# The key sum z of a linear attention: a DMA transpose through DRAM and a VectorE sum in place of two matmuls with ones

## The chip, the cores and the metric

The kernel runs on one core of one Trainium2 chip. The metric is the device time of one execution in microseconds (us), the median of several runs. The core has five engines that run their own instruction streams: TensorE (PE) for matmuls, VectorE (DVE), ScalarE (ACT), GpSimd (POOL) and SyncE (SP), which here only issues transfers (DMAs). PE writes its results to PSUM, which has eight banks of 128 x 512 fp32. "PEld" in the profile is PE's loading of weights, which runs beside its matmuls.

## The reference

An input `x` of 2048 rows (tokens) by 512 goes through two branches, which a gate mixes:

```
qkv = x @ wqkv                       # 32 heads of 16
phi(t) = where(t > 0, t + 1, exp(t)) + 1e-6
kv  = sum over s of phi(k)^T v       # per head, 16 x 16
z   = sum over s of phi(k)           # per head, 16; 512 numbers in all
a   = (phi(q) @ kv) / (phi(q) . z + 1e-6) @ wo
b   = (gelu(layernorm(x)^T-mixed by w1, b1) by w2, b2), transposed back
g   = sigmoid(sum(x * gate_w))
out = g * a + (1 - g) * b
```

The change is about `z`, the sum over all 2048 tokens of phi(k): one row of 512 numbers, which every token's denominator needs.

## The kernel before

Tokens are handled in 16 tiles of 128. All engines' instructions are pinned in program order, so the order in the file is the order on each engine and on each queue. SP issues all but three of the transfers. The transfers take eight completion counters in turn, so that each waits for the eighth transfer before it.

The stages, in the order of PE's work:

- Layer norm of the 16 tiles, and the first half of the token mixing (`accA`, seven banks, `w1A`). SP loads `x`, the weights, and `xT` (x transposed by DMA).
- `kacc`: the keys of each tile, `phi` on ACT (exponential) and DVE. Per tile DVE adds `pk` into `zacc` (L309), which so holds 128 partial sums of z, one for each partition. PE collects `Gps` = x^T phi(k). At the end ACT and DVE evict `G_sb`, and DVE splits `zacc` into two bf16 parts, `z_hi` (L333) and `z_lo` (L334).
- The block loop (from L442, `b` = 0 to 6): seven blocks `accB` of the second half of the token mixing. Between them, in `b` = 0, `kv_blocks` (32 small matmuls, 16 small DVE products with `mask`) and `z_row`; in `b` = 1 `w2_blocks`; in `b` = 0 to 3 the 16 query tiles (`q_tile`, 3, 4, 4 and 5 of them), each four matmuls, an exponential on ACT (L282) and two DVE instructions (L284, L289). Gates follow in `b` = 1 and 2, `gate_odds` in `b` = 2. From `b` = 3 on ACT runs the gelus.
- `z_row` is two matmuls: the 128 x 128 matrix `ones` by `z_hi`, then by `z_lo` into the same bank. That sums over the partitions and leaves the row z on every partition. ACT copies it to `zb` (L354).
- `normalise(t)`, four DVE instructions for each tile (L366, L371, L373, L375), the first of which reads `zb`. Each then stores its tile of `pq` to `q_dram` on SP. After every fourth tile `turn(c)` reads four transposed blocks back into `pqT`. Twelve tiles are normalised ahead of the output loop, four in it. Between them SP also loads the second half of `w2`, in two parts: `load_w2(1, 0)` after tile 2 and `load_w2(1, 7)` after tile 7 (behind `turn(1)`). The first needs the place of `w1B`, which PE gives back with the last `accB`.
- The output loop: groups of 8, 4, 3 and 1 tiles. `y_mm` (14 matmuls for each tile with `w2h`), `a_mm` (4 with `pqT`), `finish` (ACT scales into one of seven `ot` buffers, SP stores it).

All 8 PSUM banks come from one pool and are given out in the order in which they came back.

Of the kernel before, what the change touches and what calls it, by code (L numbers as in the profile page):

```python
# [9 lines left out]
ALU = mybir.AluOpType  # L10
AX = mybir.AxisListType
BF16 = mybir.dt.bfloat16
FP32 = mybir.dt.float32
# [3 lines left out]
def kernel(  # L17
# [13 lines left out]
    nc = tc.nc  # L31
    P = nc.NUM_PARTITIONS
# [7 lines left out]
    S, D = X.shape  # L40
    F = B_w1.shape[1]
    NT = S // P
    ND = D // P
# [19 lines left out]
    work = ctx.enter_context(tc.tile_pool(name="work", bufs=3))  # L63
    dpool = ctx.enter_context(tc.tile_pool(name="dpool", bufs=1, space=bass.MemoryType.DRAM))
    psum = ctx.enter_context(tc.tile_pool(name="psum", bufs=8, space=bass.MemoryType.PSUM))

    def ptile(shape, dt, name):
        return persist.tile(shape, dt, name=name, tag=name)

    def bank(name):  # L70
        return psum.tile([P, SC], FP32, name=name, tag="bank")

    def mm(o, lhsT, rhs, start, stop, **kw):
        tc.keep_in_program_order(
            nc.tensor.matmul(o, lhsT=lhsT, rhs=rhs, start=start, stop=stop, **kw)  # L75
        )
# [13 lines left out]
    zb = ptile([P, D], FP32, "zb")  # L90
# [14 lines left out]
    odds = ptile([P, NT], FP32, "odds")  # L105
    c1 = ptile([P, NT], FP32, "c1")
    c2 = ptile([P, NT], FP32, "c2")
    ones = ptile([P, P], BF16, "ones")
    zacc = ptile([P, D], FP32, "zacc")
    z_hi = ptile([P, D], BF16, "z_hi")  # L110
    z_lo = ptile([P, D], BF16, "z_lo")
    eps_t = ptile([P, 1], FP32, "eps_t")

    nc.vector.memset(eps_t[:], EPS)
# [5 lines left out]
    pin = tc.keep_in_program_order  # L120

    def load(o, i, eng=None, **kw):
        pin((eng or nc.sync).dma_start(out=o, in_=i, **kw))
# [23 lines left out]
    for c in range(NSC):  # L147
        for j in range(ND):
# [3 lines left out]
                transpose=True,  # L152
# [6 lines left out]
    for j in range(ND):  # L159
# [10 lines left out]
        out=mask[:], in_=mask[:], compare_op=ALU.is_gt, fill=1.0,  # L170
# [3 lines left out]
        out=mask[:], in_=mask[:], compare_op=ALU.is_ge, fill=0.0,  # L174
        base=0, pattern=[[-HEAD, 8], [0, HEAD]], channel_multiplier=1,
    )
    nc.gpsimd.memset(ones[:], 1.0)
    nc.gpsimd.memset(prod[:, :, HEAD : HEAD + 1], DEN_EPS)


# [57 lines left out]
    def gate(t):  # L238
        junk = work.tile([P, D], BF16, name="junk", tag="junk", bufs=1)
        tc.keep_in_program_order(  # L240
            nc.vector.tensor_tensor_reduce(  # L241
                out=junk[:], in0=xr[:, t, :], in1=gw_b[:], scale=1.0, scalar=0.0,
                op0=ALU.mult, op1=ALU.add, accum_out=gpre[:, t : t + 1],
            )
        )


    def gate_odds(t0, t1):
        pin(nc.vector.tensor_scalar_min(out=gpre[:, t0:t1], in0=gpre[:, t0:t1], scalar1=60.0))
        pin(nc.scalar.activation(out=odds[:, t0:t1], in_=gpre[:, t0:t1], func=ACT.Exp))  # L250
# [6 lines left out]
    def gelu(acc, j):  # L257
        pin(
            nc.scalar.activation(
                out=uT[:, j, :], in_=acc[:], func=ACT.Gelu_apprx_tanh,  # L260
                bias=b1_sb[:, j : j + 1], scale=1.0,
            )
        )
# [61 lines left out]
    def evict(o, acc, i):  # L325
        if i % 2 == 0:
            pin(nc.scalar.copy(out=o, in_=acc))
        else:
            pin(nc.vector.tensor_copy(out=o, in_=acc))

    for i in range(ND):
        evict(G_sb[:, i, :], Gps[i][:], i)
    pin(nc.vector.tensor_copy(out=z_hi[:], in_=zacc[:]))  # L333
    pin(nc.vector.tensor_tensor(out=z_lo[:], in0=zacc[:], in1=z_hi[:], op=ALU.subtract))  # L334


    def mlp1_block(j):
        acc = bank("accB")
        for t in range(NT):
            mlp1(acc, w1B, (j - NFA) * P, t, t == NT - 1)  # L340
        return acc

    def q_tile(t):
        qacc = bank("qacc")
        for k in range(ND):
            mm(qacc[:], xT[:, k, t * P : (t + 1) * P], wq_sb[:, k, :], k == 0, k == ND - 1)
        phi(pq[:, t, :], qacc)


    def z_row():  # L350
        zps = bank("zps")
        mm(zps[:], ones[:], z_hi[:], True, False)
        mm(zps[:], ones[:], z_lo[:], False, True)
        pin(nc.scalar.copy(out=zb[:], in_=zps[:]))  # L354

# [33 lines left out]
    def kv_blocks():  # L391
        kvps = bank("kvps")
        for j in range(ND):
            for k in range(ND):
                for p in range(0, P, 64):
                    c = j * P + p
                    mm(kvps[p : p + 64, j * 64 : j * 64 + 64], wv_sb[:, k, c : c + 64],
                       G_sb[:, k, c : c + 64], k == 0, k == ND - 1, tile_position=(0, p))

        for j in range(ND):  # L400
            for p in range(0, P, 32):
                r = (p + 32 * j) % P
                pin(
                    nc.vector.tensor_tensor(
                        out=kvbdT[r : r + 32, j, p : p + 32],
                        in0=kvps[p : p + 32, j * 64 + p % 64 : j * 64 + p % 64 + 32],
                        in1=mask[p : p + 32, p : p + 32], op=ALU.mult,
                    )
                )

    def w2_blocks():
        w2ps = [bank("w2ps") for _ in range(ND)]
        for j in range(ND):
            for p in range(0, P, 32):
                r = (p + 32 * j) % P
                mm(w2ps[j][p : p + 32, :], kvbdT[r : r + 32, j, p : p + 32],
                   wo_sb[r : r + 32, j, :], True, True, tile_position=(r, p))
        for j in range(ND):
            evict(W2sb[:, j, :], w2ps[j][:], j)
# [4 lines left out]
    def load_w2(h, f0):  # L424
        if f0 == 0:
            w2s.append(wpool.tile([P, NF, S // 2], BF16, name="w2h", tag="w"))
        load(
            w2s[h][:, f0 : f0 + 7, :],
            w2_view[:, f0 : f0 + 7, h * (S // 2) : (h + 1) * (S // 2)],
        )  # L430

    load_w2(0, 0)
    load_w2(0, 7)

    QB = 4
# [4 lines left out]
    for b in range(NFA):  # L442
        acc = mlp1_block(NFA + b)
        waiting.append((acc, NFA + b))
        if b == 0:
            kv_blocks()
            z_row()
        if b == 1:
            w2_blocks()
        if b < QB:  # L450
            for _ in range(n_q[b]):
                q_tile(qi)
                qi += 1
            for t in gates[b]:
                gate(t)
            if b == 2:
                gate_odds(0, NT)
        if b >= QB - 1:
            for a, j in waiting:
                gelu(a, j)  # L460
            waiting = []
# [27 lines left out]
            mm(yps[:, d0:d1], pqT[:, j, t * P : (t + 1) * P], W2sb[:, j, d0:d1], False, j == ND - 1)  # L489

    def finish(t, yps, d0, d1):
        ot = work.tile([P, D], BF16, name="ot", tag="ot", bufs=7)
        if t < NT - 1:
            pin(
                nc.scalar.activation(  # L495
                    out=ot[:, d0:d1], in_=yps[:, d0:d1], func=ACT.Identity,
                    scale=c1[:, t : t + 1], bias=c2[:, t : t + 1],
                )
            )
        else:  # L500
            pin(
                nc.vector.tensor_scalar(  # L502
                    out=ot[:, d0:d1], in0=yps[:, d0:d1], scalar1=c1[:, t : t + 1],
                    scalar2=c2[:, t : t + 1], op0=ALU.mult, op1=ALU.add,
                )
            )
        load(o_view[:, t, d0:d1], ot[:, d0:d1])
# [3 lines left out]
    for t0, t1 in ((0, 8), (8, 12), (12, NT - 1)):  # L511
        for t in range(t0, t1):
            held[t] = bank("yps")
            y_mm(held[t], t, 0, D)
        for t in range(t0, t1):
            a_mm(held[t], t, 0, D)
            finish(t, held[t], 0, D)
            if late and t % 2 == 1:
                normalise(late.pop(0))
                if not late:  # L520
                    turn(NSC - 1)
    t = NT - 1
    for d0, d1 in ((0, 3 * P), (3 * P, D)):
        yps = bank("yps")
        y_mm(yps, t, d0, d1)
        a_mm(yps, t, d0, d1)
        finish(t, yps, d0, d1)
# [30 lines left out]
```

## Time and profile before

| what | us |
|---|---|
| median of three runs | 163.66 (163.52 to 164.1) |
| the profiled execution | 163.69 |
| its span in the trace | 162.0 |
| PE busy | 158.3 (98%) |
| DVE busy | 116.4 (72%) |
| ACT busy | 52.9 (33%) |
| the two matmuls with ones (`zps`) | start at 61.29 and 61.51 |
| copy of `zps` to `zb` on ACT | 61.93, lasts 0.59 |
| first reader of `zb` on DVE (L366) | 88.97 |

The time of an execution is a little longer than the span, which runs from the first to the last recorded instruction. All times of day below are us from the span's start. The granted TensorE clock is full in all 40 slices of the page. The page's DMA line shows that the transfer engines are idle from about 70 to 90 us, and busy around that.

### The profile page before, as it was taken

Reading aid. Unit: us, or ns where it says so; the run is one execution under the profiler, and the core shown is the slowest. Engines: PE = TensorE matmul, PEld = TensorE weight load, DVE = VectorE, ACT = ScalarE, POOL = GpSimd, SP = SyncE. Lnnn points to the kernel's source line nnn. Section 1 sums busy time; section 2 is a strip of 40 time slices with the busy share of each in tenths; the row PEclk is TensorE's granted clock in tenths of the full one; section 3 lists DMA queues with packets and bytes.
Section 4 is the critical chain, followed back from the end, with each engine's and each line's share of the span. In section 5 each row is a group of like instructions: output and inputs, shape, how many; then the busy total and the mean of one; then the engine's idle time right before and its main releaser. Section 6 shows DMA issues by size and latency. Waiting matters only on the chain.

```text
span 162.0 us, 2203 instructions
## 1 busy us (share of the span) xinstructions
PE 158.3 (98%) x791; PEld 73.2 (45%) x791; DVE 116.4 (72%) x271; ACT 52.9 (33%) x91; POOL 1.7 (1%) x11
## 2 busy tenths in 40 slices
PE   7999999999999999999999999999999999999992
PEld 5344444444444445444444444444444444444452
DVE  2899989999999997895959999999999900000002
ACT  4222258962332125271438521000007501150040
POOL 4000000000000000000000000000000000000000
PEclk9999999999999999999999999999999999999999
DMA  5999997444799679900000107736269646647021
GB/s 142 295 336 341 327 187 162 97 98 103 233 395 375 192 243 385 390 26 0 0 0 0 36 32 233 287 76 183 65 98 318 236 97 206 215 93 146 24 97 32
DMA packets 35094, 27.54 MB, mean 170 GB/s; under 512 B 19084, under 2 KB 31500, under 8 KB 35084
## 3 DMA queue, kind: packets, MB, share of 16 engines
q1 hardware_dynamic: 34880, 27.37, 57.0%
q8 instruction: 6, 0.10, 0.3%
q10 hardware_dynamic: 204, 0.04, 0.1%
q14 instruction: 4, 0.03, 0.1%
HBM read 19.01 MB, written 4.19 MB: 143 GB/s over the span
## 4 chain that ended last, share of the span: by engine, by line
PE 98%; DVE 0%; issue 0%; DVEq 0%
PE yps L75 38%; PE accA L75 15%; PE accB L75 15%; PE qacc L75 9%; PE Gps L75 9%; PE kacc L75 9%; PE warm_ps L75 2%; PE kvps L75 0%; PE zps L75 0%; DVE ot L502 0%; PE w2ps L75 0%; PE vps L75 0%; DVEq L502 0%
## 5 line engine op out<-in xcount | busy, mean ns | idle before, releaser
L75 PE MATMUL yps<-uT,w2h 128*128 128x512 bf16 (+2 forms) x238 | 49.2, 366 | 0.0
L75 PEld LDWEIGHTS <-w2h 128*128 128x128 bf16 x238 | 22.8, 98 | 25.9
L495 ACT ACTIVATE ot<-yps,c,c 128x512 bf16<-128x512 f32 x15 | 11.7, 778 | 46.7 <-PE yps L75 37.7
L75 PE MATMUL accB<-xh,w1B 128*128 128x512 bf16 x112 | 25.0, 379 | 0.0
L75 PE MATMUL accA<-xh,w1A 128*128 128x512 bf16 x112 | 24.7, 382 | 0.0
L502 DVE TENSOR_SCALAR ot<-yps,c,c 128x384 bf16<-128x384 f32 (+1 forms) x2 | 1.1, 543 | 28.9 <-PE yps L75 28.9
L75 PEld LDWEIGHTS <-xT 128*128 128x128 bf16 x128 | 12.4, 98 | 15.1 <-issue 0.2
L75 PEld LDWEIGHTS <-w1A 128*128 128x128 bf16 x112 | 10.9, 98 | 13.4 <-issue 0.5
L75 PEld LDWEIGHTS <-w1B 128*128 128x128 bf16 x112 | 10.9, 98 | 13.2
L75 PE MATMUL kacc<-wk_sb,xT 128*128 128x512 bf16 x64 | 15.8, 379 | 0.0
L75 PE MATMUL Gps<-pk,xr 128*128 128x512 bf16 x64 | 15.8, 379 | 0.0
L75 PE MATMUL yps<-W2sb,pqT 128*128 128x512 bf16 (+2 forms) x68 | 14.6, 366 | 0.0
L75 PE MATMUL qacc<-wq_sb,xT 128*128 128x512 bf16 x64 | 14.5, 379 | 0.0
L282 ACT ACTIVATE e<-kacc 128x512 bf16<-128x512 f32 x16 | 9.2, 598 | 12.7 <-DVE pk L289 6.8
L196 DVE BATCH_NORM_STATS2 stats<-xr 128x6 f32<-128x512 bf16 (+1 forms) x19 | 11.1, 582 | 2.2 <-DMA xr<-in_A_x_dram 2.2
L375 DVE SCALAR_TENSOR_TENSOR pq<-pq,odds,rd 128x512 bf16<-128x512 bf16 x16 | 12.0, 752 | 0.6
L282 ACT ACTIVATE e<-qacc 128x512 bf16<-128x512 f32 x16 | 9.6, 597 | 7.9 <-PE qacc L75 7.3
L284 DVE TENSOR_SCALAR e<-e 128x512 bf16<-128x512 bf16 x32 | 9.2, 287 | 3.9 <-ACT e L282 3.6
L371 DVE TENSOR_REDUCE den<-prod 128x32 f32<-128x544 f32 x16 | 11.5, 720 | 0.6
L289 DVE SCALAR_TENSOR_TENSOR pk<-kacc,e 128x512 bf16<-128x512 f32 x16 | 11.1, 692 | 1.0
L289 DVE SCALAR_TENSOR_TENSOR pq<-qacc,e 128x512 bf16<-128x512 f32 x16 | 11.1, 692 | 0.6
L241 DVE CUSTOM_DVE_ANT_0 junk<-xr,gw_b 128x512 bf16<-128x512 bf16 x16 | 11.0, 690 | 0.5
(57 smaller groups left out, 94.7 us busy)
## 6 DMA issues: line engine op xcount, KB each, us to landing
w2h<-in_B_w_dram SPq DMA_DIRECT2D x4, 1792.0 KB, 8.4
w1B<-in_B_w_dram SPq DMA_DIRECT2D x4, 896.0 KB, 7.1
w1A<-in_B_w_dram SPq DMA_DIRECT2D x15, 224.0 KB, 4.1
xr<-in_A_x_dram SPq DMA_DIRECT2D x16, 128.0 KB, 3.9
q_dram<-pq SPq DMA_DIRECT2D x16, 128.0 KB, 1.8
out_dram<-ot SPq DMA_DIRECT2D x15, 128.0 KB, 1.8
wk_sb<-in_A_wqkv_dram SPq DMA_DIRECT2D x1, 512.0 KB, 7.2
wv_sb<-in_A_wqkv_dram SPq DMA_DIRECT2D x1, 512.0 KB, 13.4
```

The costliest lines, as they stand in the source:

```text
L75: nc.tensor.matmul(o, lhsT=lhsT, rhs=rhs, start=start, stop=stop, **kw)
L196: pin(nc.vector.bn_stats(out=stats[t][:, h, :], in_=xr[:, t, d0:d1]))
L241: nc.vector.tensor_tensor_reduce(out=junk[:], in0=xr[:, t, :], in1=gw_b[:], scale=1.0, scalar=0.0, op0=ALU.mult, op1=ALU.add, accum_out=gp ...
L282: pin(nc.scalar.activation(out=e[:], in_=acc[:], func=ACT.Exp))
L284: nc.vector.tensor_scalar(out=e[:], in0=e[:], scalar1=1.0, scalar2=PHI_EPS, op0=ALU.min, op1=ALU.add)
L289: nc.vector.scalar_tensor_tensor(out=o, in0=acc[:], scalar=0.0, in1=e[:], op0=ALU.max, op1=ALU.add)
L371: pin(nc.vector.tensor_reduce(out=den[:], in_=prod[:], op=ALU.add, axis=AX.X))
L375: nc.vector.scalar_tensor_tensor(out=heads, in0=heads, scalar=odds[:, t : t + 1], in1=rd[:].unsqueeze(2).to_broadcast([P, NH, HEAD]), op0= ...
L495: nc.scalar.activation(out=ot[:, d0:d1], in_=yps[:, d0:d1], func=ACT.Identity, scale=c1[:, t : t + 1], bias=c2[:, t : t + 1],)
L502: nc.vector.tensor_scalar(out=ot[:, d0:d1], in0=yps[:, d0:d1], scalar1=c1[:, t : t + 1], scalar2=c2[:, t : t + 1], op0=ALU.mult, op1=ALU.add,)
```

## The change

`z_hi` and `z_lo` become the two halves of one tile `z_parts`. Right after them (behind `load_w2(0, 7)` on the queues) `z_out` stores this tile to DRAM on ACT's queue, as 256 rows of 512, and SP reads it back in four transposes, so that column d of z lies on one partition with its 256 parts side by side. The two matmuls and ACT's copy are gone. `z_row` now stands at the end of block `b` = 2, after `gate_odds`: DVE sums each group of 256 parts into `z_cols` (128 x 4), SP stores these 512 fp32 numbers to DRAM, where they make a row, and SP loads that row to all 128 partitions of `zb`. The matrix `ones` and its memset on POOL are gone; `ot` has six buffers instead of seven, which makes room for `z_turned`.

```diff
-    ones = ptile([P, P], BF16, "ones")
-    z_hi = ptile([P, D], BF16, "z_hi")
-    z_lo = ptile([P, D], BF16, "z_lo")
+    z_parts = ptile([P, 2, D], BF16, "z_parts")
+    z_turned = ptile([P, ND, 2 * P], BF16, "z_turned")
+    z_cols = ptile([P, ND], FP32, "z_cols")
...
-    nc.gpsimd.memset(ones[:], 1.0)
...
-    pin(nc.vector.tensor_copy(out=z_hi[:], in_=zacc[:]))
-    pin(nc.vector.tensor_tensor(out=z_lo[:], in0=zacc[:], in1=z_hi[:], op=ALU.subtract))
+    pin(nc.vector.tensor_copy(out=z_parts[:, 0, :], in_=zacc[:]))
+    pin(
+        nc.vector.tensor_tensor(
+            out=z_parts[:, 1, :], in0=zacc[:], in1=z_parts[:, 0, :], op=ALU.subtract
+        )
+    )
...
+    zp_dram = dpool.tile([2 * P, D], BF16, name="zp_dram", tag="zp_dram")
+    zr_dram = dpool.tile([1, D], FP32, name="zr_dram", tag="zr_dram")
+
+    def z_out():
+        load(zp_dram[:].rearrange("(h p) d -> p h d", p=P), z_parts[:], nc.scalar)
+        for j in range(ND):
+            load(z_turned[:, j, :], zp_dram[:, j * P : (j + 1) * P], transpose=True)
+
     def z_row():
-        zps = bank("zps")
-        mm(zps[:], ones[:], z_hi[:], True, False)
-        mm(zps[:], ones[:], z_lo[:], False, True)
-        pin(nc.scalar.copy(out=zb[:], in_=zps[:]))
+        pin(nc.vector.tensor_reduce(out=z_cols[:], in_=z_turned[:], op=ALU.add, axis=AX.X))
+        load(zr_dram[:].rearrange("o (j p) -> p (o j)", p=P), z_cols[:])
+        load(zb[:], zr_dram[:].to_broadcast([P, D]))
...
     load_w2(0, 0)
     load_w2(0, 7)
+
+    z_out()
...
         if b == 0:
             kv_blocks()
-            z_row()
...
             if b == 2:
                 gate_odds(0, NT)
+                z_row()
...
-        ot = work.tile([P, D], BF16, name="ot", tag="ot", bufs=7)
+        ot = work.tile([P, D], BF16, name="ot", tag="ot", bufs=6)
```

## The prediction

> **What bounds the kernel now.** I read the page first (shares by engine, and the chain that ended last), then the timeline of PE around the change, then those of DVE and of SP, and last the transfers by window. The chain:
>
> ```profile
> PE 98%; DVE 0%; issue 0%; DVEq 0%
> ```
>
> PE is the bound from end to end: its work follows itself without a hole, so a PE instruction that goes away is worth its own pace, unless a wait that was covered comes into the open. The pace and the place, from PE's timeline:
>
> ```profile
> 60.66 0.69 PE L75 MATMUL kvps<-G_sb,wv_sb 128*64 128x64 bf16 x32
> 61.29 0.39 PE L75 MATMUL zps<-z_hi,ones 128*128 128x512 bf16 x1
> 61.51 0.38 PE L75 MATMUL zps<-z_lo,ones 128*128 128x512 bf16 x1
> 61.73 2.75 PE L75 MATMUL qacc<-wq_sb,xT 128*128 128x512 bf16 x12
> ```
>
> The recorded 0.38 is the length of a pipelined matmul; starts are 0.22 apart. From the first zps to the first qacc is 0.44 us. DVE's timeline, where the sum is put in and where `zb` is first read:
>
> ```profile
> 82.01 0.17 DVE L249 TENSOR_SCALAR gpre<-gpre 128x16 f32<-128x16 f32 x1
> 83.75 0.29 DVE L284 TENSOR_SCALAR e<-e 128x512 bf16<-128x512 bf16 x1 [1.56 <-ACT e L282]
> ...
> 88.97 0.68 DVE L366 TENSOR_TENSOR prod<-pq,zb 128x512 f32<-128x512 bf16 x1
> 89.75 0.72 DVE L371 TENSOR_REDUCE den<-prod 128x32 f32<-128x544 f32 x1
> ```
>
> There is a hole of 1.56 us after gate_odds, in which DVE waits for ACT, and ACT for PE. `zb` is read 6.8 us after that hole opens. SP's timeline:
>
> ```profile
> 56.89 1.04 SPq L123 DMA_DIRECT2D w2h<-in_B_w_dram  x2
> 91.68 5.39 SPq L123 DMA_DIRECT2D q_dram<-pq  x3
> 97.20 0.39 SPq L123 DMA_DIRECT2D w2h<-in_B_w_dram  x1
> 99.27 0.33 SPq L123 DMA_DIRECT2D q_dram<-pq  x1
> 105.17 5.06 SPq L123 DMA_TRANSPOSE pqT<-q_dram  x4
> 110.28 2.03 SPq L123 DMA_DIRECT2D q_dram<-pq  x4
> 113.71 5.03 SPq L123 DMA_TRANSPOSE pqT<-q_dram  x4
> 118.79 1.14 SPq L123 DMA_DIRECT2D w2h<-in_B_w_dram  x1
> 119.98 2.06 SPq L123 DMA_DIRECT2D q_dram<-pq  x4
> 128.89 5.04 SPq L123 DMA_TRANSPOSE pqT<-q_dram  x4
> 133.98 1.05 SPq L123 DMA_DIRECT2D out_dram<-ot  x2
> ```
>
> SP is free from 57.9 to 91.7; from there on it is one chain of stores, transposes and loads, started by `normalise`, and a late start is passed down it whole. What that chain must meet on PE is the price of a late `zb`.
>
> **Part by part.**
>
> *The two matmuls go.* Gain 0.43 us (two at 0.216, the pace of 16 accB in 3.45 us). The chain of waits books them at 0.54, by modelled ends; that is the upper end. The lower end is 0: at 67.86 the first w2ps weight load shows 0.42 us idle, put down to a DVE pq that ended at 67.72, and if PE came there 0.43 earlier and that were a true wait, all would be lost. I don't take it as one: the kvps loads show the same 0.42 before them, under the name of a transfer, so it goes with the change to small tiles. The banks say the same: they are reused in the order given back, and with zps gone w2ps takes two banks of Gps, the one of kvps and the one of the first query tile, whose last DVE read ended at 65.87. Taken: 0.43.
>
> *ACT's copy goes, a store is issued there.* The copy (0.59 at 61.93) sat in idle time. The store waits for z_lo, which ends at 60.48, and takes some 0.4 us of ACT (q_dram issues 0.33 to 0.58). Behind it on ACT is the first query exponential, at 62.79 before, 62.36 then: cover 1.4 us. Cost 0.
>
> *The four transposes on SP* wait for that store, with nothing queued behind them but z_row's own transfers. The store is 256 KB. Alone it would land like a q_dram store, 1.7 us; at worst it lands after the w2h loads, which hold the transfer engines until 69.2, plus 0.7 for its own bytes and 0.4 to land: 70.3. Four transposes at 1.26 of issue each (those of 512 rows; these have 256) put the last issue at 74.1; the pqT rows land 2.5 to 4.5 after issue, so the latest is 78.6. DVE wants them at 81.75: cover 3 us at the worst end, 11 at the best. Cost 0. Without cover DVE would stand ahead of the phis of block 3, and their banks.
>
> *The sum on DVE.* 128 x 1024 elements; the nearest row is the den reduction, 128 x 544 in 0.72, so 1.36 in proportion, 1.2 if some of the 0.72 doesn't grow; a bf16 input could be quicker. With PE 0.43 early, gate_odds ends at 81.75 and the hole closes at 83.32 (ACT shifts too). 81.75 + 1.36 = 83.11: inside. Upper end, twice the row (2.7): phis 1.1 late. The fifth query tile of the block needs the bank of its first: PE took it at 85.68, DVE gave it at 84.77, so 0.9 of cover; the next accB had 0.7 to 0.85. PE would lose 0.2 to 0.4. Taken: 0.
>
> *The row's way to `zb`.* Store and load are in series. The store: 512 elements of 4 bytes. No row has elements so small. From below, the last out_dram store (128 rows of 256 bytes) landed in 1.4. The pqT transposes, 512 packets of 256 bytes, keep the 16 transfer engines busy for about 0.75 us, some 20 ns per packet on an engine; the mean over q1 is 57% of 16 x 162 us by 34880 packets, 42 ns. 32 packets on each engine cost 0.65 to 1.35, and with 0.75 to the first byte and 0.4 from the last (read off a q_dram store) the store takes 1.8 to 2.5. I keep 60 ns for the upper end: 3.1. The load: 256 KB to 128 partitions. The w2h issued at 97.20 moved its first byte 1.15 later and landed 0.6 after its last; with 0.75 for the bytes, 2.5. So `zb` is there at 81.75 + 1.36 + 1.8 to 3.1 + 2.5 + 0.15 for two handovers = 87.6 to 88.9, taken 88.2. DVE is ready for it at 88.97 - 0.43 = 88.54, if the phis are not late. Late by -1 to +0.4: taken 0. What a lateness X would cost: normalise(2)'s store, the w2h load behind it at 97.20, turn(0), turn(1) and the last w2h load at 118.79 all go X later. That last load lands 8.7 after issue, at 127.5; PE wants its first block (f = 7 of tile 8, group from 127.81) at 129.1. So 1.6 us are free, then X counts whole. The other meetings are looser: turn(1)'s last block lands near 120.2 and is wanted at 125; turn(2)'s are wanted at 139.9, the first landed by 131.6; turn(3) starts at 141.36 and is wanted at 152.4.
>
> *The eight counters.* Seven more transfers stand ahead of the q_dram stores. Those that the stores then wait for (w2h of the first half, the z transfers) have landed by 90. Cost 0.
>
> *Six ot buffers.* ACT waited 8.1 us for the eighth `ot` until the first out store landed, at 136.06, since these stores stand behind turn(2). With six the seventh and the eighth wait: 136.06 to 136.84 and on to 137.6. SP takes them up only at some 138.6 and 139.1, and the bank of the eighth is wanted at 155. Cost 0.
>
> *Memset of ones on POOL*: at the start, nobody waits. 0.
>
> Sum, against the profiled execution: 163.69 - 0.43 = 163.26. The median before lies 0.03 lower (163.66), so 163.2.
>
> **A page against this.** The Trainium skill, "DMA: Bandwidth & Descriptors", Specifications, says that below 512 bytes a transfer engine does a read-modify-write. The out_dram rows of 256 bytes, under that limit too, landed in 1.4 us, so the trace shows no price for it; no run here has writes of 4 bytes yet. By the page the store pays for a read as well; if that were once 0.75, the store takes 3.3 and X is some 0.6, still inside the 1.6.
>
> **Rivals.**
>
> 1. *The 4-byte store drags (slower).* Mechanism: the 32 small writes on each engine go one after another, each waiting for its own trip. Price of a trip, from the tail between last byte and landing: 0.4; 32 of them 12.8, `zb` at 99.7, X = 11, loss 9.5: 172.7. Milder, 150 ns each: store 6.0, `zb` at 91.8, X = 3.2, loss 1.6, 164.8. It decides from X = 2.85 (1.6 free, 0.43 gained, 0.82 for 0.5%), which is 8.1 us for both transfers where I have 4.3 to 5.6. For it: nothing in the trace is so small. Against: 256-byte packets run at 20 ns, so they overlap. The page's rule above stands beside this rival: a read-modify-write that does not overlap would be this case.
> 2. *The gain is eaten.* By the w2ps load as above, or by a DVE sum twice as long: 163.4 to 163.7.
> 3. *z_turned late.* Landing after 81.75 holds up DVE ahead of the phis, and from 0.9 us on PE's banks. It needs 3 us more than the worst sum; 2 us beyond that costs some 1.1: 164.3.
> 4. *More is gained than the two matmuls.* Only if the change of tile shape after kvps cost PE something too; the starts, 0.22 apart before and after, show nothing. At 0.54 it is 163.1.
>
> **How the numbers follow.** 0.5% (0.82 us) is about what a measurement of this kernel can tell from no change. The forecast has 0.60, rival 2 0.13, rival 4 at its mild size 0.04, all within 0.5%; beyond 0.5% faster I leave 0.05, for a gain with no row. Rival 1 has 0.14, rival 3 0.04: slower 0.18, and so 0.77 within. The range goes from 162.8 (the upper gain of 0.54, and 0.3 of scatter, as the runs shown spread) to 164.5 (X up to 2.8, the edge of slower); it leaves out the far part of rivals 1 and 3 and the unexplained gain.
>
> **What would show it.** After kvps the next PE group is qacc, 0.22 after the last kvps; every later PE start is 0.43 earlier, with no idle PE. The sum on DVE near 81.8, 1.2 to 1.4 long, no wait on a transfer before it. The first prod at 88.5; if it waits for `zb`, the wait is X, and SP's w2h at 118.79 moves by it. The prediction is wrong if a yps of tile 8 waits for w2h, if DVE waits for z_turned, or if w2ps starts at 67.86 as before.

## The result, and the profile after

The changed kernel takes 170.18 us (median of five runs, 169.94 to 170.41) against 163.54 for the kernel before: 1.0397 times as long, with a 95% interval of 1.0377 to 1.0418. The forecast was 163.2, in a range of 162.8 to 164.5. What happened is of the kind of the first rival: the store of 512 numbers of 4 bytes drags, and `zb` comes too late.

PE is no longer the chain. From the page, section 4 of the changed kernel (shares of the span along the chain that ended last, by engine):

```profile
PE 63%; DVE 17%; DMA 14%; SPq 3%; issue 1%; ACT 0%; DVEq 0%
```

In order of time (start, duration, what), the stretch of that chain where it leaves PE:

```profile
81.61 1.23 DVE z_cols L364
82.84 0.02 issue
82.86 8.39 DMA zr_dram<-z_cols
91.25 0.02 issue
91.27 4.67 DMA zb<-zr_dram
95.94 0.02 issue
95.96 0.70 DVE prod L378
```

The sum takes 1.22 and stands where it was meant to stand. Then 2 KB take 8.39 us to DRAM and the row 4.67 us back. DVE's timeline says what that means for the first normalisation:

```profile
95.96 0.69 DVE L378 TENSOR_TENSOR prod<-pq,zb 128x512 f32<-128x512 bf16 x1 [7.49 <-DMA zb<-zr_dram]
```

DVE had been ready at 88.47; it waits 7.49 us. SP's chain, row by row the one shown of before:

```profile
98.61 5.39 SPq L124 DMA_DIRECT2D q_dram<-pq  x3
104.10 0.39 SPq L124 DMA_DIRECT2D w2h<-in_B_w_dram  x1
106.21 0.34 SPq L124 DMA_DIRECT2D q_dram<-pq  x1
112.16 5.06 SPq L124 DMA_TRANSPOSE pqT<-q_dram  x4
117.27 2.05 SPq L124 DMA_DIRECT2D q_dram<-pq  x4
122.52 5.04 SPq L124 DMA_TRANSPOSE pqT<-q_dram  x4
127.60 0.58 SPq L124 DMA_DIRECT2D w2h<-in_B_w_dram  x1
```

All rows down to the second group of q_dram stores are 6.9 to 7.0 later than before (7.49, less the half microsecond by which PE and DVE came early). The second turn is 8.81 later (122.52 for 113.71), and so is the last w2h load (127.60 for 118.79). PE's timeline shows both arriving too late:

```profile
120.33 3.62 PE L75 MATMUL yps<-W2sb,pqT 128*128 128x512 bf16 x16
125.14 0.39 PE L75 MATMUL yps<-W2sb,pqT 128*128 128x512 bf16 x1 [1.19 <-DMA pqT<-q_dram]
126.45 0.39 PE L75 MATMUL yps<-W2sb,pqT 128*128 128x512 bf16 x1 [0.93 <-DMA pqT<-q_dram]
127.86 0.61 PE L75 MATMUL yps<-W2sb,pqT 128*128 128x512 bf16 x1 [1.01 <-DMA pqT<-q_dram]
129.09 5.19 PE L75 MATMUL yps<-W2sb,pqT 128*128 128x512 bf16 x13 [0.62 <-DMA pqT<-q_dram]
134.12 12.41 PE L75 MATMUL yps<-uT,w2h 128*128 128x512 bf16 x56
```

Tile 4 waits 3.75 us in four pieces for the blocks of turn(1). After that 13 matmuls take 5.19 us, 0.40 each instead of 0.22: the granted clock in the stretch 129 to 134 is 0.54 of full speed. Then the weight loads of tile 8 reach f = 7 and wait for the last w2h load:

```profile
133.90 1.39 PEld L75 LDWEIGHTS <-w2h 128*128 128x128 bf16 x7
135.78 1.19 PEld L75 LDWEIGHTS <-w2h 128*128 128x128 bf16 x7 [0.48 <-DMA w2h<-in_B_w_dram]
```

That load was issued at 127.60, so it landed 8.2 later. (f counts the 14 blocks of `w2h` that each tile needs; blocks 7 to 13 of tiles 8 to 15 come with the last load.) Before, f = 7 of tile 8 started near 129.3 (127.81 and seven times 0.216), with no wait; here it starts near 135.9. The difference is 6.6, and the spans differ by 6.5 (168.5 and 162.0): the last w2h load sets the end.

It does so by a small margin. Without this wait f = 7 would have started near 135.6 (134.12 and seven times 0.216), because the four waits for pqT and the slow clock had already cost PE nearly as much; the page's chain accordingly runs through turn(1) and not through this load. So two late arrivals meet within 0.3 us, and both come from the late start of SP's chain. A quicker PE would only have waited longer at f = 7, and an earlier w2h load alone would have gained 0.3.

### The profile page after: what moved, and what is told of

Same layout as the page of the kernel before. It is cut to its first block, busy times and chain, and to the rows that moved or that the text cites. A ratio compares the mean times of both kernels' runs of the same rounds, so it can differ in the third digit from the quotient of the medians.

```text
span 168.5 us, 2205 instructions
## 1 busy us (share of the span) xinstructions
PE 160.6 (95%) x789; PEld 73.3 (44%) x789; DVE 117.8 (70%) x272; ACT 52.1 (31%) x90; POOL 1.5 (1%) x10
## 4 chain that ended last, share of the span: by engine, by line
PE 63%; DVE 17%; DMA 14%; SPq 3%; issue 1%; ACT 0%; DVEq 0%
PE yps L75 22%; PE accA L75 14%; PE kacc L75 8%; PE Gps L75 8%; PE accB L75 6%; DMA zr_dram<-z_cols 5%; PE qacc L75 4%; DVE pq L387 4%; DVE den L383 4%; DVE prod L378 3%; SPq L124 3%; DMA zb<-zr_dram 3%; DMA w1A<-in_B_w_dram 2%; DMA q_dram<-pq 2%; DVE rd L385 2%; DVE pq L289 2%
## 5 line engine op out<-in xcount | busy, mean ns | idle before, releaser
L75 PE MATMUL yps<-W2sb,pqT 128*128 128x512 bf16 (+2 forms) x68 | 17.8, 409 | 3.8 <-DMA pqT<-q_dram 3.8
L378 DVE TENSOR_TENSOR prod<-pq,zb 128x512 f32<-128x512 bf16 x16 | 11.0, 685 | 7.5 <-DMA zb<-zr_dram 7.5
L75 PEld LDWEIGHTS <-pqT 128*128 128x128 bf16 x68 | 7.0, 106 | 13.8 <-DMA pqT<-q_dram 5.3
## 6 DMA issues: line engine op xcount, KB each, us to landing
xr<-in_A_x_dram SPq DMA_DIRECT2D x16, 128.0 KB, 4.1
q_dram<-pq SPq DMA_DIRECT2D x16, 128.0 KB, 1.9
out_dram<-ot SPq DMA_DIRECT2D x15, 128.0 KB, 1.8
```

Source lines behind the costliest of these rows:

```text
L378: nc.vector.tensor_tensor(out=prod[:, :, 0:HEAD], in0=heads, in1=by_head(zb[:]), op=ALU.mult)
```

## The experiments

Theory 1: the two matmuls were worth what PE's starts say, everything else in the change is hidden, and the loss is the lateness of `zb` passed down SP's chain. Its rivals: the new transfers or the smaller `ot` disturb the rest, or the gain is eaten at w2ps. A second question is why 2 KB take 8.4 us.

### Each part alone

`no_zps`: before, with the matmuls and the copy taken out and nothing put in.

```diff
     def z_row():
-        zps = bank("zps")
-        mm(zps[:], ones[:], z_hi[:], True, False)
-        mm(zps[:], ones[:], z_lo[:], False, True)
-        pin(nc.scalar.copy(out=zb[:], in_=zps[:]))
+        pass
...
+    nc.gpsimd.memset(zb[:], 2048.0)
```

> Before without the two matmuls with ones and ACT's copy: zb is a constant set at the start, so z is left out of the result and nothing is put in its place. This is what the removal alone is worth. Theory 1 (the change's gain is the two matmuls, its loss is the late zb): 0.43 to 0.54 us less than before, 163.0 to 163.2. Rival (the gain is eaten by a wait at w2ps): as before, 163.5 to 163.7.

Measured: 163.51, 0.9982 of before (0.9969 to 0.9995); span 161.4. The gain is there and is small: the median lies above the expected 163.0 to 163.2, and the interval allows a gain of 0.1 to 0.5 us. In the profile kvps starts at 60.47 and the first qacc at 61.09, 0.62 apart where before it was 1.07: 0.45 us. The w2ps group starts at 67.24, so no wait there eats it.

`ot6_alone`: before, with `bufs=6` for `ot`.

> Before with six ot buffers instead of seven, nothing else. Theory 1: the seventh output tile waits like the eighth did, and nobody waits for it: as before, 163.4 to 163.8. Rival (the buffers are part of the loss): 164 or more.

Measured: 163.75, ratio 0.9999 (0.9986 to 1.0012). The buffers cost nothing.

`shadow`: the changed kernel with the whole DMA route kept, but `zb` from the matmuls (`ones` and its memset are back).

```diff
...
-        load(zb[:], zr_dram[:].to_broadcast([P, D]))
+        load(zacc[:], zr_dram[:].to_broadcast([P, D]))
...
+    def z_ones():
+        zps = bank("zps")
+        mm(zps[:], ones[:], z_parts[:, 0, :], True, False)
+        mm(zps[:], ones[:], z_parts[:, 1, :], False, True)
+        pin(nc.scalar.copy(out=zb[:], in_=zps[:]))
...
             kv_blocks()
+            z_ones()
```

> The changed kernel with all its transfers, its sum and its six buffers, but zb again comes from the two matmuls; the row of z that the DMAs bring is loaded to zacc, which nobody reads then. Theory 1: nobody waits for the row, so as before, 163.4 to 163.9. Rival (the new transfers or the sum disturb the other work by themselves): 165 to 170.

Measured: 163.79, ratio 1.0004 (0.9991 to 1.0016). The row of z takes as long as in the changed kernel (store 8.6, load 5.1), and it costs nothing as long as nobody waits for it. SP, which sits behind the store until 91.89, issues the first q_dram store at 92.34 instead of 91.68, and that is hidden too. So the transfers are harmless; the wait is the loss.

### How much for how late

`p1_before_gates2`: in the changed kernel, `z_row` ahead of the two gates of block 2.

```diff
+            if b == 2:
+                z_row()
             for t in gates[b]:
                 gate(t)
             if b == 2:
                 gate_odds(0, NT)
-                z_row()
```

> The changed kernel with z_row ahead of the two gates of block 2 instead of behind gate_odds, so about 1.6 us earlier on DVE. Theory 1: zb is there at 94.4 instead of 95.96, and all of the 1.6 comes back: 168.4 to 168.8. Rival (the loss doesn't hang on when zb comes): 170.2 as the changed kernel.

Measured: 168.96, ratio 1.0318 (1.0299 to 1.0338), span 167.0. `zb` is waited for 5.90 us, 1.59 less; the span is 1.5 less (by the medians 1.2, so that 168.96 lies just above the expected 168.4 to 168.8). Theory 1 holds, nearly one for one. Here too it is w2h that ends the wait: issued at 126.01, and PE stands until 134.30.

```profile
132.04 1.67 PE L75 MATMUL yps<-uT,w2h 128*128 128x512 bf16 x7
134.30 10.75 PE L75 MATMUL yps<-uT,w2h 128*128 128x512 bf16 x48 [0.59 <-DMA w2h<-in_B_w_dram]
```

`p2_after_gates1`: `z_row` a whole block earlier.

```diff
+            if b == 1:
+                z_row()
             if b == 2:
                 gate_odds(0, NT)
-                z_row()
```

> The changed kernel with z_row at the end of block 1 instead of block 2. DVE reaches it at 74.5 and waits for z_turned until about 75.0; 1.2 of sum, 8.4 of store and 4.7 of load bring zb at 89.4, 0.9 after DVE is ready for it. Theory 1: that is within the 1.6 us which SP's chain has to spare, so the gain of the matmuls shows: 163.0 to 163.3, faster than before. If nothing is to spare: 164.0. Rival (not the lateness): 170.

Measured: 163.45, ratio 0.9984 (0.9972 to 0.9995), span 161.6. DVE still waits 0.93 us for `zb`, and PE for nothing; the gain of the matmuls is all there. One moved line takes the change from 4% slower to a shade quicker than before.

`p3_zout_first`: `z_out` ahead of the two w2h loads, and `z_row` ahead of the gates of block 1.

```diff
+    z_out()
     load_w2(0, 0)
     load_w2(0, 7)
-    z_out()
...
+            if b == 1:
+                z_row()
             for t in gates[b]:
                 gate(t)
...
-                z_row()
```

> The changed kernel with z_out ahead of the two w2 loads on the queues, so that the parts are turned by about 70, and z_row ahead of the gates of block 1 (DVE at 73.1). The sum ends at 74.3; store 8.4 and load 4.7 bring zb at 87.5, ahead of DVE's need at 88.5; the w2 loads move some 10 us later, to about 79, and are wanted at 96. Theory 1: 163.0 to 163.2, with no wait for zb. If the store suffers from the w2 loads beside it, zb at 90 or later and 163.1 to 164.

Measured: seven executions from 164.0 to 165.74 with a median of 164.87, ratio 1.0074 (1.0048 to 1.0100), and two more of 167.91 and 168.28, which no trace here explains. The first expectation missed; the second (163.1 to 164) came nearer and was passed too. The parts were stored in 2.2 us instead of 7.7, as meant, but the w2h loads then ran beside the row's store until about 81, and that store landed after 12.8 us: nearly all its small packets are recorded after 79, when these loads run out, and it landed 6.3 after the last. `zb` is waited for 2.32 us in the profiled execution (164.0), in which PE waits 0.17 for w2h: just past what is free.

The profiled executions side by side, in us. X is DVE's wait for `zb`; the third column is SP's issue of the last w2h load, the fourth PE's time lost to waits for pqT and w2h:

| kernel | X | last w2h | PE waits | span |
|---|---|---|---|---|
| before | 0 | 118.79 | 0 | 162.0 |
| no_zps | 0 | 118.33 | 0 | 161.4 |
| p2_after_gates1 | 0.93 | 119.31 | 0 | 161.6 |
| p3_zout_first | 2.32 | 121.60 | 0.17 | 162.3 |
| p1_before_gates2 | 5.90 | 126.01 | 3.15 | 167.0 |
| changed | 7.49 | 127.60 | 3.75 | 168.5 |

The last w2h load is free up to some 121 (118.79 + 2.3); from there on the end moves with it. In the changed kernel the half clock adds some 3 us to the 3.75 of waits; the short stand at f = 7 does not show as a wait of PE's matmuls.

### Why the store takes 8.4 us

The transfer engines are through with this store long before it lands. In the changed kernel it is issued at 82.86; by stretch (the last two numbers are the busy share of the 16 engines and GB/s):

```profile
83.50:84.00 0.50, 0.50 (x4) 0.21 (x3) 0.50 (x1) 0.50 (x1) 0.00 (x0) 1.00 0.34 3
84.00:85.00 1.00, 1.00 (x7) 0.46 (x5) 0.96 (x3) 0.60 (x1) 0.00 (x0) 1.00 0.09 1
85.00:86.00 1.00, 1.00 (x6) 0.42 (x5) 0.96 (x4) 0.60 (x2) 0.00 (x0) 1.00 0.00 0
```

All its packets lie between 83.8 and 84.2, and it lands at 91.25, 7.1 after the last of them. Up to then the engines move nothing but one instruction fetch at 90; in `p2_after_gates1`, where no fetch falls into this stretch, the store took 8.6 all the same. So the price is not paid packet by packet on the engines, but between the last packet and the landing. The runs below ask what it goes by.

`s16_runs`: the changed kernel, in place, with the store's 512 numbers in 128 runs of four.

```diff
-        load(zr_dram[:].rearrange("o (j p) -> p (o j)", p=P), z_cols[:])
+        load(zr_dram[:].rearrange("o (p j) -> p (o j)", p=P), z_cols[:])
```

> The changed kernel with z_cols stored in 128 runs of 16 bytes instead of 512 of 4, in place and otherwise alike; the 512 numbers of z then lie in another order, so the result's denominators are wrong. If the store's price goes by the number of writes it lands in about 3, zb is there at 90.6, 2.1 after DVE is ready, and the time is 163.5 to 164.3. If any small write costs the same, 170.2 as the changed kernel. If the loss is not the late zb, 170.2 too, with the store short.

Measured: 163.56, ratio 0.9987 (0.9975 to 0.9999). The store lands in 2.5, 1.5 after its last packet, and the load in 3.3:

```profile
83.42 0.35 SPq L124 DMA_DIRECT2D zr_dram<-z_cols  x1
85.97 0.34 SPq L124 DMA_DIRECT2D zb<-zr_dram  x1
...
89.33 0.69 DVE L378 TENSOR_TENSOR prod<-pq,zb 128x512 f32<-128x512 bf16 x1 [0.30 <-DMA zb<-zr_dram]
```

The same 2 KB from the same place at the same point; only the layout in DRAM differs, and the whole loss is gone. But fewer writes and longer writes changed together. Three kernels measure stores by themselves, in a chain behind the last output in which each transfer waits for the one ahead, so that the gap between two starts on SP is the landing time. Each of them ran once.

`m_stores`:

```diff
...
+    four = zacc[:, 0:ND]
...
+    def back(src):
+        load(zacc[:], src.to_broadcast([P, D]))
...
+    load(m4[:].rearrange("o (j p) -> p (o j)", p=P), four)
+    back(m4[:])
+    load(m16[:].rearrange("o (p j) -> p (o j)", p=P), four)
+    back(m16[:])
+    load(mfar[:].rearrange("(j p) c -> p j c", p=P)[:, :, 0:1], zacc[:, 0:ND].unsqueeze(2))
...
+    load(m128[:].rearrange("o p -> p o"), zacc[:, 0:1])
...
+    load(m512[:], zacc[:, 0:P])
...
```

> Before, with a chain of transfers behind the last output, each waiting for the one ahead (the span grows by their sum; nothing of the result changes): m4, 512 writes of 4 bytes as the changed kernel's store of z, then read back as one row to 128 partitions; m16, the same 2 KB in 128 runs of 16 bytes, read back the same way; mfar, 512 writes of 4 bytes each in a 512-byte line of its own, read back as 512 reads of 4 bytes; m128, 128 writes of 4 bytes in one 512-byte line; m512, 128 rows of 512 bytes. If the price goes by the number of writes: m4 and mfar 8.4, m16 and m128 some 3. If it comes from several small writes to the same line: m4 8.4, mfar 2 to 3, m128 3 to 8. If any write this small is slow once: m4, m16, m128, mfar alike near 8. m512 some 1.7 in each case. The row's load took 4.7 in the changed kernel: the same after m16 if it is the repeated row, less if it is what the 4-byte writes left behind.

SP's timeline of this kernel, with m4, m16, mfar, m128 and m512 in this order, each followed by its load back:

```profile
159.99 0.42 SPq L123 DMA_DIRECT2D m<-zacc  x1
170.00 0.32 SPq L123 DMA_DIRECT2D zacc<-m  x1
174.23 0.32 SPq L123 DMA_DIRECT2D m<-zacc  x1
175.63 0.32 SPq L123 DMA_DIRECT2D zacc<-m  x1
179.66 0.37 SPq L123 DMA_DIRECT2D mfar<-zacc  x1
181.65 0.37 SPq L123 DMA_DIRECT2D zacc<-mfar  x1
183.56 0.33 SPq L123 DMA_DIRECT2D m<-zacc  x1
190.95 0.33 SPq L123 DMA_DIRECT2D zacc<-m  x1
```

512 writes of 4 bytes in their places in the row: 10.0, as the first of the chain (8.4 in `m_groups` below). 512 writes of 4 bytes, each 512 bytes from the next: 2.0. From the last packet to the landing these are 8.7 and 0.7. So neither the number of writes nor their size alone makes the price; it comes when they lie beside each other. 128 writes in one line of 512 bytes (m128) take 7.4, 128 runs of 16 bytes (m16) 1.4, and 128 rows of 512 bytes 1.5. The second case of the expectation holds. The row's load took 4.2 after m4 and 4.0 after m16.

`m_pitch` varies the distance: 128 numbers, one from each partition, at a pitch of 16 to 512 bytes, then 8 bytes and 4 bytes side by side; then rows of x.

```diff
...
+    def spaced(n, w):
+        d = dpool.tile([P, w], FP32, name=n, tag=n)
+        load(d[:, 0:1], row[:, 0:1])
+        load(row[:, 0:1], d[:, 0:1])
+    spaced("q16", 4)
...
+    load(w8[:], row[:, 0:2])
...
+    load(w4[:], row[:, 0:1])
...
+    load(xr[:, 0, :], x_view[:, 0, :])
+    load(xr[:, 0, :], X[0:1, :].to_broadcast([P, D]))
...
```

> Before with another chain behind the last output, each transfer waiting for the one ahead; nothing of the result changes. 128 writes of 4 bytes at a pitch of 16, 32, 64, 128 and 512 bytes (q16 to q512), of 8 bytes side by side (w8), of 4 bytes side by side (w4), each read back; then x's rows: 128 different rows to 128 partitions, one row to all 128, and both again. If writes to the same small line queue up, the time falls as the pitch grows and jumps to 2 where each write has a line of its own: w4 7.4, w8 some 4, and the pitch at which it reaches 2 is the line. If it is only that writes under 16 bytes that touch each other are slow, q16 is already at 2. For the row: if a repeated row costs more than different rows, it lands 1 to 2 later (4 against 2.5); if not, both take the same and zb's 4.7 was the time of any load of this size.

By the gaps on SP: pitch 16 took 2.5 (first in the chain, behind the last output's store), 32, 64, 128 and 512 bytes 1.4 each, 8 bytes side by side 3.3, 4 bytes side by side 7.1. So the price falls with the distance and is gone at 32 bytes, which is the first case of the expectation. One row of x (1 KB) to all partitions landed in 3.1, 128 different rows right after it in 2.0: a repeated row costs about 1 more. The first pair of these is not clean, since the chain let the first load overlap with the one ahead.

`m_groups` repeats the doubtful points, not at the head of the chain, and varies the number of partitions:

```diff
...
+    def spaced(n, w, c, parts=P):
+        d = dpool.tile([P, w], FP32, name=n, tag=n)
+        load(d[0:parts, 0:c], row[0:parts, 0:c])
+        load(row[0:parts, 0:c], d[0:parts, 0:c])
+    spaced("r512", 128, 1)
+    spaced("r16", 4, 1)
+    spaced("r8", 2, 1)
+    spaced("t4all", 1, 1)
+    spaced("t4of64", 1, 1, 64)
+    spaced("t4of32", 1, 1, 32)
+    spaced("t8all", 2, 2)
...
```

> Before with a third chain behind the last output, each transfer waiting for the one ahead; nothing of the result changes. In m_pitch the store at a pitch of 16 stood first and took 2.5, and may have waited for the last output's store. Now r512 stands first, then 4 bytes at a pitch of 16 (r16) and of 8 (r8), 4 bytes side by side from 128, 64 and 32 partitions (t4all, t4of64, t4of32), 8 bytes side by side (t8all), the change's own store (m4) and 32 bytes side by side (g8). If writes that share 16 bytes wait for each other, r16 1.4, r8 and t8all 3.3 (one wait of 1.9), t4all 7.1 (three), m4 7 to 9, g8 1.4, and the number of partitions doesn't matter: t4of64 and t4of32 near 7. If the price goes by the number of small writes to a region, t4of64 about 4.3 and t4of32 about 2.8. If the line is 32 bytes, r16 is at 2.5 again.

SP's timeline, each store followed by its load back (here r16, r8, t4all, t4of64, t4of32):

```profile
163.51 0.32 SPq L123 DMA_DIRECT2D r<-zacc  x1
165.71 0.32 SPq L123 DMA_DIRECT2D zacc<-r  x1
167.38 0.32 SPq L123 DMA_DIRECT2D r<-zacc  x1
170.45 0.32 SPq L123 DMA_DIRECT2D zacc<-r  x1
172.97 0.32 SPq L123 DMA_DIRECT2D t4all<-zacc  x1
179.82 0.32 SPq L123 DMA_DIRECT2D zacc<-t4all  x1
183.75 0.50 SPq L123 DMA_DIRECT2D t4of<-zacc  x1
190.53 0.46 SPq L123 DMA_DIRECT2D zacc<-t4of  x1
193.99 0.33 SPq L123 DMA_DIRECT2D t4of<-zacc  x1
197.27 0.31 SPq L123 DMA_DIRECT2D zacc<-t4of  x1
```

r512 1.6, r16 2.2, r8 3.1, t8all 2.9, t4all 6.9, t4of64 6.8, t4of32 3.3, the change's store again 8.4, 32 bytes side by side 1.4. No case of the expectation holds whole. Half of the partitions cost the same, so the price isn't the number of writes; a quarter of them costs half, so "each 16 bytes for itself" isn't the whole of it either; and r16 at 2.2 leans to the third case, a line of 32 bytes. A reading that fits most numbers: writes that one transfer engine puts into the same 16 bytes land one after another, at some 1.8 each (1.4 + 1.8 is near r8 and t8all, 1.4 + 3 x 1.8 = 6.8 is t4all and t4of64), and with 32 partitions an engine has two such neighbours instead of four. That engines share out partitions in this way was not shown here, and r16 at 2.2 instead of 1.4 does not fit. What is shown is the price by layout.

### A version that keeps the gain

`best16`: `z_row` at the end of block 1, runs of 16 bytes, and `normalise` reading `zb` in the order in which it now lies.

```diff
...
-                out=prod[:, :, 0:HEAD], in0=heads, in1=by_head(zb[:]), op=ALU.mult
+                out=prod[:, :, 0:HEAD].rearrange("p (j h) e -> p j h e", j=ND),
+                in0=pq[:, t, :].rearrange("p (j h e) -> p j h e", j=ND, e=HEAD),
+                in1=zb[:].rearrange("p (h e j) -> p j h e", j=ND, e=HEAD), op=ALU.mult
...
```

> The changed kernel with z_row at the end of block 1, z_cols stored in 128 runs of 16 bytes, and normalise reading zb in the matching order (its 512 numbers with a step of four), so that nothing is left out. The sum ends at 76.0, the store takes 1.4 to 2.5, the load 3.3 to 4.7: zb at 81 to 83, well ahead of 88.5. Theory 1: the gain of the two matmuls and no wait: as with no_zps, 163.0 to 163.5, 0.998 of before. If reading zb with a step slows the product (0.68 each, sixteen of them), the chain from 91.7 stretches and some of it is lost: 163.5 to 164.5.

Measured: 163.6, ratio 0.9994 (0.9980 to 1.0008), nothing gained. The second case came true: no wait for `zb`, but each product now takes 1.07 instead of 0.68, the last w2h load goes out at 120.90, and PE's weight loads wait 0.51 for it.

```profile
88.63 1.07 DVE L378 TENSOR_TENSOR prod<-pq,zb 128x512 f32<-128x512 bf16 x1
```

`best16_copy`: the same, but one copy brings the row into order, and `normalise` is as before.

```diff
...
+    def z_order():
+        pin(
+            nc.vector.tensor_copy(
+                out=zb[:].rearrange("p (j q) -> p j q", j=ND),
+                in_=zacc[:].rearrange("p (q j) -> p j q", j=ND),
+            )
+        )
...
             if b == 2:
                 gate_odds(0, NT)
+                z_order()
```

> As best16, but the row of z goes to zacc and DVE brings it into order in zb with one copy behind gate_odds of block 2, in the hole of 1.56 us there; normalise reads zb without a step as before. Nothing is left out. If the step was all that cost best16 its gain, the products are back at 0.68 and the time is that of no_zps, 0.998 of before, 163.0 to 163.5; if the copy (0.7 to 1.1) overruns the hole, at most 0.3 more and still within what SP's chain has to spare.

Measured: 163.55, ratio 0.9982 (0.9971 to 0.9994), the ratio of `no_zps`: the full gain, which is 0.2%. The copy takes 0.62 in the hole.

```profile
81.87 0.62 DVE L370 COPY zb<-zacc 128x512 f32<-128x512 f32 x1 [0.24 <-DMA zacc<-zr_dram]
83.19 0.29 DVE L284 TENSOR_SCALAR e<-e 128x512 bf16<-128x512 bf16 x1 [0.70 <-ACT e L282]
```

## Why the prediction was wrong

- **The step that failed: "the row's way to zb", and in it the 0.4 us "from the last (read off a q_dram store)" to the landing.** Store and load together were sized at 4.3 to 5.6 us and measured 13.1; the store (1.8 to 3.1 forecast) took 8.4. Its sum had three parts. The first byte (0.75) and the packets (0.65 to 1.35) were near or too dear: the packets began 0.9 after the issue and took 0.4. The tail of 0.4 measured 7.1. It was read off a store of rows of 1 KB, and the runs show that it goes by the layout: 0.7 when 512 small writes lie apart, 6.3 to 8.7 when they lie beside each other. The upper end was made by a dearer packet (60 ns, my own choice), so the range left the term that grew at one value. No row of before held neighbouring writes under 256 bytes.
- **The load** was the second mis-sized term: 4.7 for 2.5. Its first packet came 2.4 after the issue instead of 1.15, and its packets took 1.9 instead of 0.75. The w2h load from which I read the latency has different rows; a repeated row measured about 1 us more than different rows. The load took 3.2 to 4.0 after runs of 16 bytes and 3.6 to 5.1 after this store; what holds it up there stays open.
- **Rival 1** had the right outcome and the wrong machinery. Its two cases, 164.8 and 172.7, lie on either side of the 170.2 measured. It had the 32 writes on each engine go one after another at 0.15 or 0.4 each, but the engines were through with all of them in 0.4 us, and 512 such writes that lie apart land in 2.0. What drags is the landing of writes that lie beside each other. It had 0.14; with an upper bound taken honestly as unknown it should have had far more.
- **The Trainium skill's read-modify-write rule** ("DMA: Bandwidth & Descriptors", Specifications) was weighed as one extra trip. Here 4-byte writes carry a large price only where they meet: 32 bytes or more apart they land in 1.4 to 2.0, about as quickly as rows of 512 bytes (1.5), beside each other from 128 partitions in 7 to 10. Whether a read-modify-write is the cause, no run here shows.
- **What a lateness costs: right in kind, with two sizes off.** The free part was put at 1.6; by the last w2h load it is 2.3, since that load landed in 8.2 rather than 8.7. And X isn't passed down bare: SP's chain starts 7.0 later, but turn(1) came 8.81 late. The fourth q_dram store of that group landed 3.6 after its issue, where in p2_after_gates1, s16_runs and p3_zout_first it took 1.8. The transfer windows show an instruction fetch of some 16 KB in this stretch in the two kernels in which it was slow (changed, p1_before_gates2), and in the changed kernel a trickle of 18 packets in about 1 us at its end, as if of one transfer engine alone. The same stretch of before, shadow and the three just named has no such fetch. That the fetch held up this engine's share of the store is argued from that, not tried. With both, 7.0 + 1.8 - 2.3 is the 6.5 measured; by the prediction's rule an X of 7.49 would have made 169.2 (163.26 + 7.49 - 1.6), where the profiled execution took 170.22.
- **The meetings.** Turn(1) was called looser than w2h (4.8 us to spare). It was the first to be missed, because 8.81 is more than both; w2h still came last and set the end, as said, but by no more than 0.3 us.
- **The two matmuls: right.** 0.43 forecast; the starts from kvps to the next group moved by 0.44, and `no_zps` gained 0.0018 of 163.7, 0.3 us (0.1 to 0.5). w2ps moved with it (67.28 for 67.86) and again has 0.42 us of idle before it, so a wait did not make the 0.42 us there, as argued.
- **The sum on DVE: right**, 1.22 for 1.2 to 1.36, inside the hole. **The transposes: right**; the last was issued at 72.6 and landed at 75.0, in a forecast of up to 78.6, and DVE's sum shows no wait for it. **ACT's store and the six buffers: right**, no cost.
- **Not foreseen: the clock.** The profile before granted full speed in every slice, and the forecast had no term for it. It didn't decide, but together with the waits for pqT it would have kept the end within 0.3 us of where it is, had the last w2h load come earlier.

## What to carry to other kernels

Before a transfer with elements of a few bytes is put on a path that something waits for, ask how the elements lie in DRAM: runs of 16 bytes from each partition landed in 1.4 to 2.9, the same bytes in 4-byte pieces that interleave between partitions in 8.4 to 10, and one DVE copy of 0.62 put the order right afterwards. A route through DRAM of unknown length belongs a whole stage ahead of its reader, which cost nothing here, where the queue was idle; one moved line was worth 4%. A store whose packets have ended hasn't landed yet: here it took 7 us more. And where no row of a profile resembles an operation, its price has no upper bound from that profile, and the range must say so.

## What the runs showed of the hardware that was not expected

- Stores to DRAM of 4 bytes: side by side from 128 partitions 6.9 to 7.4, from 64 6.8, from 32 3.3; at a pitch of 8 bytes 3.1, of 16 2.2 to 2.5, of 32 and more 1.4 to 1.6. Side by side with 8 bytes 2.9 to 3.3, with 16 and 32 bytes 1.4. The same numbers read back from 4 bytes side by side took 3.5 to 3.9, at a pitch of 16 and more 1.5 to 1.9.
- The 512 numbers of z in their row: 6.3 to 8.7 from the last packet on the transfer engines to the landing. With w2h loads running beside it the whole store took 12.8 (p3_zout_first).
- The granted TensorE clock fell to half with waits of at most 1.2 us. PE waits 1.19, 0.93, 1.01 and 0.62 us, with one matmul between each two; the clock is at half before the third wait is over. PE's busy time, matmuls and granted clock by stretch (the clock is the third number from the end):

```profile
123.00:125.00 2.00, 0.94 (x5) 0.21 (x3) 1.93 (x4) 1.59 (x3) 0.00 (x0) 1.00 0.29 66
125.00:127.00 2.00, 0.78 (x2) 0.19 (x2) 1.93 (x4) 0.00 (x0) 0.00 (x0) 0.94 0.54 123
127.00:129.00 2.00, 0.61 (x1) 0.10 (x1) 1.90 (x5) 0.00 (x0) 0.00 (x0) 0.50 0.44 85
131.00:133.00 2.00, 2.00 (x6) 0.70 (x5) 1.93 (x4) 0.78 (x1) 0.00 (x0) 0.50 0.99 332
133.00:135.00 2.00, 2.00 (x10) 0.81 (x9) 1.93 (x4) 0.00 (x0) 0.00 (x0) 0.85 0.97 335
```

A mean of 0.94 over 125 to 127 puts the fall near 126.8, and one of 0.85 over 133 to 135 the rise near 133.6: 6.8 us at half. In `p1_before_gates2`, after waits of 0.73, 0.94 and 0.89, it was at half from about 128.0 to 131.4, 3.4 us. The Trainium skill ("TensorE: Matmul & The Clock Gate", Part 1) has the clock fall to half after an idle window of some 3.4 us and rise again after about as much work. The half speed agrees; but no wait here was longer than 1.2 us, so the idle time need not be in one piece.
